# The scale of ScalarE's linear factor from a register in place of a pointer operand

## The chip, the cores and the metric

The kernel runs on one core of a Trainium2 chip. The time is that of the device in microseconds (us), from runs of the whole program; less is better. The engines are TensorE (PE; its weight loads are PEld), VectorE (DVE), ScalarE (ACT), GpSimd (POOL) and SyncE (SP). Each has its own queue of instructions and runs it in order; the engines wait for each other by semaphores.

## The reference

A polynomial attention is followed by a layer with a rational activation. Attention has 4 batches of 4 heads, 1088 tokens and a head width of 32, so the layer sees 4352 tokens of width 128 and has 2048 hidden columns.

```python
def phi(x):
    a = np.einsum('rd,bhsd->bhsr', S1, x)
    b = np.einsum('rd,bhsd->bhsr', S2, x)
    return np.einsum('bhsi,bhsj->bhsij', a, b).reshape(*x.shape[:-1], r * r)
q_p, k_p = (phi(q), phi(k))
kv = np.einsum('bhsf,bhsd->bhfd', k_p, v)
z = np.sum(k_p, axis=2)
num = np.einsum('bhsf,bhfd->bhsd', q_p, kv)
den = np.einsum('bhsf,bhf->bhs', q_p, z)[..., None] + 1e-06
...
h = x @ w_in
h2 = h * h
h3 = h2 * h
P = a[0] + a[1] * h + a[2] * h2 + a[3] * h3
Q = 1.0 + np.abs(b[0]) * np.abs(h) + np.abs(b[1]) * h2
g = P / (Q + 1e-06)
return (g @ w_out).astype(np.float32)
```

## The kernel before, in words

Nothing loops on the chip: the program is a straight list of instructions, written out by the string `ORDER`, one step per word (`name:index`), and each engine gets its part of the steps in that order. Two kinds of work are interleaved. The attention part makes, per batch, the summed key products (`kvz`) and then, per block of some 384 queries, the attention output, transposed into `xT`. The layer part takes 17 units, numbered 0 to 16, of 4096 columns (a unit is a stretch of tokens times a share of the 2048 hidden columns, laid side by side), most of them worked on in two halves of 2048 columns, the last in a half and two quarters of 1024.

The steps of a unit:

- `h` (L455, TensorE): the product of `w_in` and `xT` into the PSUM tile `h_ps` of 1024 columns, of which there are two; `e` (L461, ScalarE) copies it to `hh` in SBUF as bf16.
- `u`, `w`, `y` (L484, L490, L495, VectorE): |h| and then w = |h| (|b1| |h| + |b0|), so that the denominator is 1 + w.
- `ln` (L546) and `ex` (L550), both on ScalarE: r = exp(-ln(1 + 1e-6 + w)), the reciprocal of the denominator.
- `pa` (L541, ScalarE) or `pd` (L536, VectorE): the linear factor p = a3 h + a2. The table `P_ON_ACT` says for each half which engine makes it: ScalarE makes 23 of them, 21 of 2048 columns and 2 of 1024, VectorE 12.
- `s`, `m`, `v`, `x` (L554, L558, L564, L569, VectorE): s = h r and the terms with h s and p, in the tile `g`.
- `G` (L588, TensorE): r, s and g times three copies of `w_out` scaled by a0, a1 and 1 (made once, in the steps `wo`, L621 to L625), summed over the hidden columns in PSUM; `st` (L597, L605) transposes the sum and stores it.

The four values of a lie in `a_sb`, a tile of 128 partitions by 4 in which every partition holds the same four numbers (it is fetched by a DMA that reads the four numbers 128 times); the two of b lie in `b_sb`, fetched next on the same queue. `a1`, `a2` and `a3` are columns of `a_sb`, one value per partition. In `a_p` ScalarE's instruction therefore reads two operands of one value per partition beside its data: the scale a3 and the bias a2. The activations of `ln` and `ex` have constants in their place.

The step `ba` stands once in `ORDER`, between `kp0` and `kp1` of the first batch; there ScalarE takes the absolute values of b (L682). The next ScalarE step behind it is `kk`, the copies of the key products into `kvz` (L312).

Of the kernel before, what the change touches and what calls it, by code (L numbers as in the profile page):

```python
# [15 lines left out]
ACT = mybir.ActivationFunctionType  # L16
# [53 lines left out]
def kernel(  # L70
# [13 lines left out]
    nc = tc.nc  # L84
# [54 lines left out]
    for i, s_in in enumerate((S1, S2)):  # L139
# [5 lines left out]
                      in_=bass.AP(tensor=k.tensor, offset=k.offset, ap=[[S * D // 32, 128], [W, NM], [1, 4 * D]]))  # L145
    nc.sync.dma_start(out=k0[:, 0:km].rearrange("p (m x) -> p m x", m=NM - 1)[:, :, 4 * D:],
                        in_=k0_src[:, 0:km].rearrange("p (m x) -> p m x", m=NM - 1)[:, :, 4 * D:])
# [4 lines left out]
    a_sb = consts.tile([128, 4], FP, name="a_sb")  # L152
# [14 lines left out]
    def turn(i, cols=512):  # L167
        idle_ps = bank()
        for _ in range(TURNS[i]):
            nc.tensor.matmul(idle_ps[:, :cols], lhsT=idle[:, 0:128], rhs=idle[:, :cols], start=True, stop=True)  # L170
# [45 lines left out]
    b_abs = consts.tile([128, 2], FP, name="b_abs")  # L216
    ab0, ab1 = b_abs[:, 0:1], b_abs[:, 1:2]
    a1, a2, a3 = a_sb[:, 1:2], a_sb[:, 2:3], a_sb[:, 3:4]
    w_sb = [big.tile([128, nf, d_model], BF, name=f"w_out_{i}") for i in range(3)]
    XR = 2048  # L220
    xT = big.tile([d_model, XR], FP, name="xT")
# [277 lines left out]
    def part_of(i, key, h):  # L499
        n = 2 if key == "p" else 4  # L500
        t = rings[key].rearrange("p n x -> p (n x)")
        if h == "both":
            return t[:, 2 * i % n * HW:2 * i % n * HW + UW]
        z = (2 * i + (h > 0)) % n * HW
        return t[:, z + (h - 2) * PW:z + (h - 1) * PW] if h > 1 else t[:, z:z + HW]
# [9 lines left out]
    def on_act(i, h):  # L515
        return P_ON_ACT[2 * i + (h > 0)]

    def skip(wide=(), same=None):
        def wrap(f):
            def step(i, h):  # L520
                if i in wide and i not in QUARTER and (same is None or same(i, 0) == same(i, 1)):
                    if h != 1:
                        return
                    h = "both"
                if h in (0, "both") or (h > 1) == (i in QUARTER):
                    f(i, h, live[i]["hh"][:, span(h)])
            return step
        return wrap

    def first(h):  # L530
        return 0 if h == "both" else h
# [6 lines left out]
    @skip(WIDE_P, on_act)  # L538
    def a_p(i, h, hh):
        if on_act(i, first(h)):  # L540
            nc.scalar.activation(out=part_of(i, "p", h), in_=hh, func=ACT.Identity, scale=a3, bias=a2)  # L541

    @skip()
    def a_ln(i, h, hh):
# [47 lines left out]
    def store(i):  # L592
        t0, tl, f0, per = units[i]
        if f0 + per < nf:
            return
        o = mid.tile([128, TC], FP, name="out_sb")
        nc.vector.transpose(out=o[:, :tl], in_=outs[t0][:, :tl])  # L597
        c = t0
        while c < t0 + tl:
            b = c // S  # L600
            ce = min(t0 + tl, (b + 1) * S)
            o_b = out[b * S:(b + 1) * S, :].rearrange("(g j) d -> g j d", g=32)
            j0, j1 = (c - b * S) // 32, (ce - b * S) // 32
            for e in range(d_model // 32):
                (nc.scalar if t0 + tl == n_tok and e % 2 else nc.sync).dma_start(  # L605
                    out=o_b[:, j0:j1, e * 32:(e + 1) * 32],
                    in_=o[e * 32:(e + 1) * 32, c - t0:ce - t0].rearrange("p (j d) -> p j d", d=32))
            c = ce
# [8 lines left out]
    def w_part(x):  # L617
        y, f = x // 2, x % 2 * (nf // 2)
        o, t = w_sb[y][:, f:f + nf // 2], w_out_sb_f[:, f:f + nf // 2]
        if y == 2:  # L620
            (nc.scalar.copy if W_ENG[x] else nc.vector.tensor_copy)(out=o, in_=t)  # L621
        elif W_ENG[x]:
            nc.scalar.activation(out=o, in_=t, func=ACT.Copy, scale=a_sb[:, y:y + 1])
        else:
            nc.vector.tensor_scalar(out=o, in0=t, scalar1=a_sb[:, y:y + 1], scalar2=None, op0=AX.mult)  # L625
# [26 lines left out]
    def fetch_x(x):  # L652
# [5 lines left out]
    blocks = [lambda: QA, lambda: QB, lambda: QC, once(lambda: Spread(0, q0, cuts[3], cuts[4]))]  # L658
    blocks += [once(lambda b=b, c0=c0, c1=c1: Spread(b, fetched["lq", b], c0, c1)) for b in range(1, B) for c0, c1 in spans]
    does = {"e": evac, "h": hidden, "u": d_abs, "w": d_w, "y": d_y, "ln": a_ln, "ex": a_exp, "pa": a_p, "pd": d_p,  # L660
            "s": d_s, "m": d_hs, "v": d_v, "x": d_g, "G": gather}
    q_does = {"qt": "transposes", "qs": "sketches", "qc": "copies", "qf": "features", "qp": "products", "qd": "plus",
# [5 lines left out]
    for step in ORDER:  # L668
        name, i = step.split(":")
        i = int(i)  # L670
        if name in q_does:
            getattr(blocks[i](), q_does[name])()
        elif name in k_does:
            getattr(keys[i](), k_does[name][0])(*k_does[name][1:])
        elif name == "wo":
            w_part(i)
        elif name in loads:
            fetched[name, i] = loads[name](i)
        elif name == "tn":
            turn(i)  # L680
        elif name == "ba":
            nc.scalar.activation(out=b_abs, in_=b_sb, func=ACT.Abs)  # L682
        elif name == "st":
            store(i)
        else:
            does[name[:-1]](i, int(name[-1]))
# [31 lines left out]
```

## Time and profile before

| | us |
|---|---|
| median of 3 runs | 272.32 |
| runs from, to | 272.06, 272.9 |
| span of the profiled execution, from its first instruction to its last | 270.8 |
| busy TensorE, VectorE, ScalarE in that span | 257.7, 256.7, 248.8 |
| the 23 instructions of L541 together | 46.7 |

The profile is that of one execution; no other time of that execution is given than its span, and the span is 1.5 us below the median of the runs. Its lines name the source line (L541), the engine, the operation and out<-in by the program's names, with partitions x elements and types. In a group, "x21" is the number of instructions, then come the busy time in us and the mean duration of one in ns, then the idle time of the engine just before them and what ended it. In a timeline a line starts with the start and the duration in us. A recorded duration reaches past the start of the next instruction on the same engine by up to about 0.1 us, so the distance between starts is the better measure of what an instruction costs its engine.

### The profile page before, as it was taken

Reading aid. Unit: us, or ns where it says so; the run is one execution under the profiler, and the core shown is the slowest. Engines: PE = TensorE matmul, PEld = TensorE weight load, DVE = VectorE, ACT = ScalarE, POOL = GpSimd, SP = SyncE. Lnnn points to the kernel's source line nnn. Section 1 sums busy time; section 2 is a strip of 40 time slices with the busy share of each in tenths; the row PEclk is TensorE's granted clock in tenths of the full one; section 3 lists DMA queues with packets and bytes.
Section 4 is the critical chain, followed back from the end, with each engine's and each line's share of the span. In section 5 each row is a group of like instructions: output and inputs, shape, how many; then the busy total and the mean of one; then the engine's idle time right before and its main releaser. Section 6 shows DMA issues by size and latency. Waiting matters only on the chain.

```text
span 270.8 us, 3732 instructions
## 1 busy us (share of the span) xinstructions
PE 257.7 (95%) x1382; PEld 147.5 (54%) x1397; DVE 256.7 (95%) x278; ACT 248.8 (92%) x224; POOL 2.9 (1%) x24
## 2 busy tenths in 40 slices
PE   8999999999999899999999999999999999999683
PEld 3787556864645344635464554444545356675372
DVE  3777999999999999999999999999999999999994
ACT  1268999998999999999999999999999999999991
POOL 4000000000000000000000000000000000000000
PEclk9999999999999999999999999999999999999889
DMA  6995614333230044231304000400034200020005
GB/s 167 265 323 151 156 38 136 117 90 96 76 106 34 12 118 100 77 75 33 97 6 123 7 0 3 119 11 0 15 97 73 43 0 0 2 39 1 0 2 79
DMA packets 30530, 19.55 MB, mean 72 GB/s; under 512 B 20400, under 2 KB 26672, under 8 KB 30512
## 3 DMA queue, kind: packets, MB, share of 16 engines
q1 hardware_dynamic: 28864, 18.92, 26.9%
q10 hardware_dynamic: 1648, 0.40, 0.8%
q8 instruction: 11, 0.18, 0.3%
q14 instruction: 7, 0.06, 0.1%
HBM read 16.16 MB, written 3.15 MB: 71 GB/s over the span
## 4 chain that ended last, share of the span: by engine, by line
ACT 47%; PE 34%; issue 8%; DVE 5%; DMA 4%; SPq 0%; ACTq 0%; DVEq 0%
PE h_ps L455 16%; ACT ln L546 13%; ACT r L550 12%; ACT hh L461 12%; PE att_ps L588 10%; ACT p L541 7%; PE att_ps L365 3%; DMA v_sb<-in_v_dram 2%; PE att_ps L302 2%; DMA k_sb<-in_k_dram 2%; DVE g L558 2%; DVE s L554 1%; ACT xT L398 1%; PE att_ps L391 1%; PE att_ps L409 1%
## 5 line engine op out<-in xcount | busy, mean ns | idle before, releaser
L455 PE MATMUL h_ps<-xT,w_in_sb 128*128 128x512 f32 (+1 forms) x320 | 125.8, 537 | 2.8 <-ACT hh L461 1.9
L455 PEld LDWEIGHTS h_ps<-xT,w_in_sb 128*128 128x128 f32 x320 | 58.3, 190 | 55.2 <-issue 37.3
L461 ACT CAST hh<-h_ps 128x1024 bf16<-128x1024 f32 x68 | 67.5, 1027 | 3.5 <-PE h_ps L455 3.1
L588 PEld LDWEIGHTS <-w_out 128*128 128x128 bf16 x460 | 45.5, 100 | 45.9 <-issue 14.3
L546 ACT ACTIVATE ln<-w 128x2048 f32<-128x2048 bf16 (+1 forms) x35 | 66.0, 1887 | 0.7 <-DVE w L495 0.6
L550 ACT ACTIVATE r<-ln 128x2048 bf16<-128x2048 f32 (+1 forms) x35 | 65.8, 1880 | 0.6 <-PE att_ps L588 0.2
L541 ACT ACTIVATE p<-hh,a_sb 128x2048 bf16<-128x2048 bf16 (+1 forms) x23 | 46.7, 2035 | 0.1
L554 DVE TENSOR_TENSOR s<-hh,r 128x2048 bf16<-128x2048 bf16 (+2 forms) x33 | 41.0, 1246 | 0.2 <-ACT r L550 0.2
L495 DVE TENSOR_TENSOR w<-w,u 128x4096 bf16<-128x4096 bf16 (+2 forms) x22 | 39.4, 1798 | 0.1
L588 PE MATMUL att_ps<-g,w_out 128*128 128x512 bf16 (+1 forms) x154 | 34.8, 350 | 4.3 <-DVE g L569 3.9
L558 DVE TENSOR_TENSOR g<-hh,s 128x2048 bf16<-128x2048 bf16 (+1 forms) x30 | 35.2, 1175 | 0.0
L569 DVE TENSOR_TENSOR g<-g,p 128x2048 bf16<-128x2048 bf16 (+1 forms) x30 | 35.1, 1178 | 0.1
L588 PE MATMUL att_ps<-r,w_out 128*128 128x512 bf16 (+1 forms) x154 | 34.8, 353 | 0.3
L588 PE MATMUL att_ps<-s,w_out 128*128 128x512 bf16 (+1 forms) x137 | 29.3, 342 | 0.2
L490 DVE TENSOR_SCALAR w<-u,b_abs 128x4096 bf16<-128x4096 bf16 (+2 forms) x22 | 23.8, 1090 | 0.0
L484 DVE TENSOR_SCALAR u<-hh 128x4096 uint16<-128x4096 uint16 (+2 forms) x22 | 21.4, 976 | 1.6 <-ACT hh L461 1.5
L365 PEld LDWEIGHTS att_ps<-kvz,q_pT 128*128 128x128 f32 x144 | 17.7, 191 | 4.6 <-issue 2.0
L365 PE MATMUL att_ps<-kvz,q_pT 128*128 128x66 f32 x144 | 17.9, 273 | 0.1
L302 PEld LDWEIGHTS att_ps<-v_sb,k_p 128*64 128x64 f32 (+1 forms) x288 | 8.8, 138 | 1.9 <-DVE qT L325 0.8
L536 DVE TENSOR_SCALAR p<-hh,a_sb 128x2048 bf16<-128x2048 bf16 x12 | 9.7, 808 | 0.0
L302 PE MATMUL att_ps<-v_sb,k_p 128*64 128x64 f32 (+1 forms) x288 | 9.2, 223 | 0.5 <-DMA v_sb<-in_v_dram 0.5
L273 DVE TENSOR_TENSOR k_p<-att_ps,b_sk 128x1024 f32<-128x1024 f32 (+2 forms) x8 | 9.3, 1178 | 0.1
(60 smaller groups left out, 134.3 us busy)
## 6 DMA issues: line engine op xcount, KB each, us to landing
a_all<-sk_d SPq DMA_DIRECT2D x6, 384.0 KB
b_all<-sk_d SPq DMA_DIRECT2D x12, 192.0 KB
v_sb<-in_v_dram SPq DMA_DIRECT2D x12, 144.0 KB
k_sb<-in_k_dram SPq DMA_DIRECT2D x3, 544.0 KB
q_sb<-in_q_dram SPq DMA_DIRECT2D x3, 544.0 KB
a_all<-sk_d SPq DMA_DIRECT2D x4, 320.0 KB
b_all<-sk_d SPq DMA_DIRECT2D x8, 160.0 KB
w_out_sb_f<-in_moe_w_out_dram SPq DMA_DIRECT2D x2, 512.0 KB
```

The costliest lines, as they stand in the source:

```text
L365: nc.tensor.matmul(self.nd[:, o:o + 2 * KW], lhsT=self.q_p[:, c, x:x + 128], rhs=kvz[self.b % 2][:, c, :], start=True, stop=True)
L455: nc.tensor.matmul(t[:, x * tl:(x + 1) * tl], lhsT=w_in_sb[:, f * 128:(f + 1) * 128], rhs=xT[:, x_at(t0):x_at(t0) + tl], start=True, stop= ...
L461: nc.scalar.copy(out=live[i]["hh"][:, part * PW:(part + 1) * PW], in_=live[i]["h", part])
L490: nc.vector.tensor_scalar(out=t[:, c], in0=live[i]["u"][:, c], scalar1=ab1, scalar2=ab0, op0=AX.mult, op1=AX.add)
L495: nc.vector.tensor_mul(out=t[:, c], in0=t[:, c], in1=live[i]["u"][:, c])
L541: nc.scalar.activation(out=part_of(i, "p", h), in_=hh, func=ACT.Identity, scale=a3, bias=a2)
L546: nc.scalar.activation(out=t, in_=live[i]["w"][:, span(h)], func=ACT.Ln, bias=1.0 + 1e-6)
L550: nc.scalar.activation(out=part_of(i, "r", h), in_=live[i]["ln"], func=ACT.Exp, scale=-1.0)
L554: nc.vector.tensor_mul(out=part_of(i, "s", h), in0=hh, in1=part_of(i, "r", h))
L558: nc.vector.tensor_mul(out=part_of(i, "g", h), in0=hh, in1=part_of(i, "p" if horner(i, first(h)) else "s", h))
L569: nc.vector.tensor_mul(out=g, in0=g, in1=part_of(i, "s" if horner(i, first(h)) else "p", h))
L588: nc.tensor.matmul(outs[t0][:, :tl], lhsT=w_sb[y][:, f0 + x, :], rhs=part_of(i, key, h)[:, c:c + tl], start=done[0] == 0, stop=done[0] == ...
```

## The change

One register of ScalarE is allocated. In the step `ba`, behind the absolute values of b, it is loaded with the 32 bits of a3 from the first partition of `a_sb`. The activation in `a_p` takes its scale from that register; its bias a2 stays an operand of one value per partition. VectorE's form of the same factor (`d_p`), the order of the steps and all DMAs stay.

```diff
@@ -216,6 +216,7 @@
     b_abs = consts.tile([128, 2], FP, name="b_abs")
     ab0, ab1 = b_abs[:, 0:1], b_abs[:, 1:2]
     a1, a2, a3 = a_sb[:, 1:2], a_sb[:, 2:3], a_sb[:, 3:4]
+    a3_reg = nc.scalar.alloc_register("a3_reg")
     w_sb = [big.tile([128, nf, d_model], BF, name=f"w_out_{i}") for i in range(3)]
     XR = 2048
     xT = big.tile([d_model, XR], FP, name="xT")
@@ -538,7 +539,7 @@
     @skip(WIDE_P, on_act)
     def a_p(i, h, hh):
         if on_act(i, first(h)):
-            nc.scalar.activation(out=part_of(i, "p", h), in_=hh, func=ACT.Identity, scale=a3, bias=a2)
+            nc.scalar.activation(out=part_of(i, "p", h), in_=hh, func=ACT.Identity, scale=a3_reg, bias=a2)
 
     @skip()
     def a_ln(i, h, hh):
@@ -680,6 +681,7 @@
             turn(i)
         elif name == "ba":
             nc.scalar.activation(out=b_abs, in_=b_sb, func=ACT.Abs)
+            nc.scalar.reg_load(a3_reg, a_sb[0:1, 3:4].bitcast(mybir.dt.int32))
         elif name == "st":
             store(i)
         else:
```

## The prediction

> **What bounds the kernel now.** I read first the page's busy times, then busy time by stretch of the span, then the chain of waits, then who waits for whom, and last the timelines of ScalarE and VectorE. The first fence has the page's busy line, the two stretches 20 to 248 us and 248 to 271 us (busy us of each engine, in brackets its instructions), and the chain by engine and by line.
>
> ```profile
> span 270.8 us, 3732 instructions
> PE 257.7 (95%) x1382; PEld 147.5 (54%) x1397; DVE 256.7 (95%) x278; ACT 248.8 (92%) x224; POOL 2.9 (1%) x24
> 20.00:248.00 228.00, 224.38 (x1121) 123.90 (x1135) 224.98 (x225) 225.52 (x196) 0.00 (x0) 1.00 0.24 61
> 248.00:271.00 23.00, 15.01 (x99) 10.16 (x98) 18.76 (x23) 16.03 (x12) 0.00 (x0) 0.93 0.16 24
> ACT 47%; PE 34%; issue 8%; DVE 5%; DMA 4%; SPq 0%; ACTq 0%; DVEq 0%
> by line: PE h_ps L455 16.2%; ACT ln L546 13.0%; ACT r L550 12.1%; ACT hh L461 12.1%; PE att_ps L588 10.2%; issue 8.1%; ACT p L541 7.4%; PE att_ps L365 3.1%; DMA v_sb<-in_v_dram 2.4%; PE att_ps L302 1.7%; DMA k_sb<-in_k_dram 1.6%; DVE g L558
> ```
>
> The page's 92% for ScalarE hides the point. Its idle time lies at the start and the end; in the 228 us between, ScalarE is idle for 228.00 - 225.52 = 2.5 us, VectorE for 3.0 and TensorE for 3.6. Three engines are full there. The chain of waits therefore crosses between them: 47% ScalarE, 34% TensorE. After 248 us VectorE has the most work (18.76 us, ScalarE 16.03).
>
> Next, who waits for whom from 20 to 250 us (total us, times, longest).
>
> ```profile
> PE h_ps L455 <- ACT hh L461: 1.9, 4, 0.8
> PE h_ps L455 <- ACT xT L398: 0.4, 1, 0.4
> DVE u L484 <- ACT hh L461: 1.5, 2, 0.9
> DVE rec L380 <- ACT den L376: 0.9, 2, 0.5
> DVE s L554 <- ACT r L550: 0.2, 1, 0.2
> ACT hh L461 <- PE h_ps L455: 3.1, 3, 1.7
> ACT r L550 <- PE att_ps L588: 0.2, 1, 0.2
> ```
>
> VectorE loses 1.5 + 0.9 + 0.2 = 2.6 us to ScalarE, TensorE 1.9 + 0.4 = 2.3 us, and ScalarE itself loses 3.3 us to TensorE. That is all that a faster ScalarE could take from the other two, and part of it lies where no earlier ScalarE instruction is touched.
>
> **The change part by part: the pointer removed.** Here are ScalarE's groups with shapes kept apart: busy us, mean ns of one, idle before.
>
> ```profile
> L541 ACT ACTIVATE p<-hh,a_sb 128x2048 bf16<-128x2048 bf16 x21 | 44.3, 2112 | 0.1
> L546 ACT ACTIVATE ln<-w 128x2048 f32<-128x2048 bf16 x33 | 63.9, 1937 | 0.6 <-DVE w L495 0.6
> L541 ACT ACTIVATE p<-hh,a_sb 128x1024 bf16<-128x1024 bf16 x2 | 2.4, 1226 | 0.0
> L550 ACT ACTIVATE r<-ln 128x1024 bf16<-128x1024 f32 x2 | 2.1, 1051 | 0.0
> L623 ACT ACTIVATE w_out<-w_out_sb_f,a_sb 128x1024 bf16<-128x1024 f32 x2 | 2.3, 1156 | 0.0
> L621 ACT CAST w_out<-w_out_sb_f 128x1024 bf16<-128x1024 f32 x1 | 1.1, 1070 | 0.0
> ```
>
> p (L541) reads two pointers, the scale a3 and the bias a2; ln and r have constants alone. The difference is 2112 - 1937 = 175 ns on 2048 columns and 1226 - 1051 = 175 ns on 1024: a fixed price of two pointers, whatever the width. One pointer alone shows in the w_out pair, which differ in a pointer scale on the same shape: 1156 - 1070 = 86 ns. So the price adds up pointer by pointer, and 175 / 2 = 88 ns is what one p should lose. There are 21 + 2 = 23 of them: 23 x 88 ns = 2.0 us of ScalarE's time. No row shows a scale from a register, so this value stands between two ends: the register is as cheap as a constant (-2.0 us in all) or handled as dearly as the pointer or more (0 and above, the third rival). I take the first, because the value is known to the engine's queue before the instruction starts and no SBUF read of 128 values is left.
>
> The saving must also be in the distance between starts and not only in the recorded length, since neighbours overlap:
>
> ```profile
> 246.02 2.10 ACT L541 ACTIVATE p<-hh,a_sb 128x2048 bf16<-128x2048 bf16 x1
> 248.02 1.91 ACT L546 ACTIVATE ln<-w 128x2048 f32<-128x2048 bf16 x1
> 207.49 1.93 ACT L546 ACTIVATE ln<-w 128x2048 f32<-128x2048 bf16 x1
> 209.30 1.01 ACT L461 CAST hh<-h_ps 128x1024 bf16<-128x1024 f32 x1
> 201.93 1.91 ACT L546 ACTIVATE ln<-w 128x2048 f32<-128x2048 bf16 x1
> 203.87 1.91 ACT L550 ACTIVATE r<-ln 128x2048 bf16<-128x2048 f32 x1
> ```
>
> From p to the next start 2.00 us pass, from an ln to an independent next start 1.81 us: 0.19 us for two pointers, so the whole price is in the pitch. The third pair (r needs ln) has 1.94 us: where the next instruction can't overlap, 0.13 us are lost.
>
> **How much of 2.0 us reaches the end.** The chain has 7.4% of 270.8 us on p, 20.0 us, or 10 instructions of 2.0 us. Were the chain to stay where it is, the end would move by 10 x 88 ns = 0.88 us; with the other engines full it switches sooner, so 0.88 us is the upper end of the likely case. The lower end is 0. Two places show both signs:
>
> ```profile
> 246.90 1.22 DVE L558 TENSOR_TENSOR g<-hh,s 128x2048 bf16<-128x2048 bf16 x1
> 248.16 1.23 DVE L558 TENSOR_TENSOR g<-hh,p 128x2048 bf16<-128x2048 bf16 x1
> 162.14 0.23 DVE L380 RECIPROCAL rec<-den 128x12 f32<-128x12 f32 x1 [0.38 <-ACT den L376]
> 158.27 1.98 PE L455 MATMUL h_ps<-xT,w_in_sb 128*128 128x512 f32 x4 [0.44 <-ACT hh L461]
> 91.95 5.80 PE L455 MATMUL h_ps<-xT,w_in_sb 128*128 128x512 f32 x12 [0.85 <-ACT hh L461]
> ```
>
> At 248.16 VectorE starts the product with p as p ends (246.02 + 2.10 = 248.12), 0.04 us after its own work at 246.90 + 1.22 = 248.12, where neighbours normally overlap by 0.08: at most 0.12 us is to be had there. At 162.14 (0.38 us idle, 0.46 with the overlap) and 158.27 (0.44 us) VectorE and TensorE do wait for ScalarE, so what ScalarE has gained by then passes on. But VectorE's idle time there and what lies behind it leave little: 0.46 + 0.12 is what I find from 158 us on, and of the earlier waits (91.95 among them) I count some 0.2 us, since hh is late from TensorE, too (3.1 us of waits), and each such place takes ScalarE's lead away again. Sum as an upper figure: 0.2 + 0.46 + 0.12 = 0.78 us; as each wait gives only what ScalarE leads by then, I take two thirds: 0.5 us. That is 270.8 - 0.5 = 270.3 us of span. The profiled span is 1.5 us below the median of the runs, 272.32 us; with the same 1.5 us around it the forecast is 271.8 us.
>
> **The register load added.** It is one instruction on ScalarE's queue, behind b_abs (L682). No row shows such a load. Nearest rows: a sequencer-only semaphore event (51 ns), and ScalarE's only other load of its own state, the table load (1283 ns). What stands behind it on the queue is the copy into kvz:
>
> ```profile
> 10.12 0.21 ACT L682 ACTIVATE b_abs<-b_sb 128x2 f32<-128x2 f32 x1
> 12.34 0.54 ACT L312 COPY kvz<-att_ps 64x33 f32<-64x33 f32 x4 [2.02 <-PE att_ps L302]
> L455 PEldq EVENT_SEMAPHORE  x5: 51/51/51, 16.8 to 218.5; - x5
> L158 ACT ACT_TABLE_LOAD x1 | 1.3, 1283 | 3.6 <-DMA s_raw<-in_S_dram 3.6
> ```
>
> kvz waits 2.02 us for TensorE's products, so both ends, 0.05 and 1.28 us, are hidden: 0. Without that cover the load's own length would go on ScalarE's path, up to 1.28 us, and the copy to kvz, then TensorE's first query products, would be late. a_sb was fetched before b_sb on the same queue, so no new DMA wait arises. The Trainium skill, Runtime: NRT & Kernel Launch, section Instruction fetch mechanics, gives some 200 ns for one register loaded from HBM; by that figure the load is hidden as well, and no run here shows it.
>
> No wait is added to any p: the register is written once, on the engine that reads it. The DMAs, the order and the other queues stay as they are.
>
> **The rivals.**
>
> 1. *More comes through* (faster). ScalarE leads for longer than I give it: the waits of 2.6 and 2.3 us on ScalarE are large enough to take all of 2.0 us, and 47% of the chain is on ScalarE. Against it: the chain has only 10 of 23 p's, and VectorE's 18.76 us after 248 us don't hang on ScalarE. It gives 0.9 to 2.0 us, say 1.2: 271.1 us.
>
> 2. *The register costs what the pointer cost* (no change). The edit then does not do what it is said to, as ScalarE handles both forms alike: 272.3 us. If the bits were read as an integer, the time would be the forecast's and the output wrong.
>
> 3. *The register form cannot be prepared behind its predecessor* (slower). Fetching the register's value then falls between two activations, at each of the 23 p's on a full engine. The price: the overlap lost, 0.13 us, and one sequencer step, 0.05 us, against 0.088 us saved: +0.09 us each, 23 x 0.09 = 2.1 us. It decides from 0.088 us per p. As ScalarE has 2.5 us idle in 228, nearly all of it would be on the path, say 1.7 us: 274.0 us. A far end is a DMA issue on ScalarE's queue (two in 0.88 us, so 0.44 each): 23 x 0.35 = 8.1 us. For it: no row has this form. Against it: ScalarE starts tiny copies 0.06 us after the one before, so its queue is filled ahead.
>
> ```profile
> 42.22 0.19 ACT L376 ACTIVATE den<-att_ps 128x12 f32<-128x12 f32 x1
> 42.28 1.07 ACT L621 CAST w_out<-w_out_sb_f 128x1024 bf16<-128x1024 f32 x1
> 267.62 0.88 ACTq L605 DMA_DIRECT2D out_dram<-out_sb  x2
> ```
>
> The Trainium skill's Perfetto Trace Analysis, section Sequencer Loop, says that an engine instruction is pushed into a queue and only rarely gets special work in the sequencer's own code. A register operand may be such a rare case: with it the sum would be that of this rival, and without it that of the forecast. The 0.06 us between starts above bear out the queue, and no row of before bears out the special work.
>
> 4. *The load isn't hidden*: it takes longer than 2.02 us or holds up the start in another way, about 1.3 us: 273.6 us.
>
> **How the numbers follow.** Forecast (0.5 us less) 0.45; more comes through 0.25; register as dear as the pointer 0.12; slower by lost overlap 0.15; load in the way 0.03. The time is the forecast's, 271.8 us; its own range is 271.1 to 272.5. The range that holds 8 in 10 takes in most of the first rival (to 1.6 us less: 270.7) and the nearer half of the third (to 1.5 us more: 273.8). About 0.3%, 0.8 us, is what a measurement of this kernel tells from no change: three runs of before spread over 0.84 us. Faster by more than that: 0.23 of the first rival, 0.05 of the forecast's upper end and 0.02 by scatter, 0.30. Slower: 0.14 + 0.03 and 0.03 by scatter, 0.20. Within: 0.50.
>
> **What would show it right or wrong.** In the changed profile the 21 wide p's should have a mean near 2024 ns and the two narrow ones near 1138; a start-to-start distance of 1.91 us after p. If p stays at 2112 ns, rival 2 holds; if the mean falls but the gap before p grows, or its idle before rises from 0.1 us to over 1 us, rival 3. ScalarE's busy time should fall by 2.0 us to 246.8, and its idle from 20 to 248 us rise by about 1.5 us, put down to TensorE or VectorE: that is the part absorbed. kvz should still start at 12.3 us, waiting for TensorE; a start past 13 us is rival 4. A span below 269.9 us, or VectorE's waits on ScalarE falling by over 1 us, would mean that I underrated what passes on.

## The result and the profile after

| | before | after |
|---|---|---|
| median, us | 272.34 (8 runs, 272.06 to 272.9) | 271.81 (8 runs, 271.45 to 272.05) |
| ratio, 95% interval | | 0.9972 [0.9961, 0.9982] |
| profiled execution: its time, its span, us | not given, 270.8 | 272.05, 270.3 |
| L541 (after: L542), 23 instructions together, us | 46.7 | 44.5 |

The medians differ by 0.53 us. The ratio of the runs says 0.28%, which is 0.76 us, with 0.49 to 1.06 us as its interval; where comparisons are set beside each other below, it is by the ratio. The source lines behind the first edit are one higher than before, those behind the register load two.

First the page of the changed kernel and its two stretches 20 to 248 us and 248 to 271 us (busy us of each engine, in brackets its instructions; then the clock, the DMA share and GB/s).

```profile
span 270.3 us, 3749 instructions
PE 257.8 (95%) x1397; PEld 147.5 (55%) x1397; DVE 256.2 (95%) x278; ACT 247.2 (91%) x224; POOL 2.9 (1%) x24
20.00:248.00 228.00, 224.98 (x1139) 124.22 (x1138) 225.08 (x226) 224.91 (x197) 0.00 (x0) 1.00 0.24 61
248.00:271.00 23.00, 14.78 (x98) 9.98 (x96) 18.17 (x22) 15.07 (x11) 0.00 (x0) 0.87 0.16 24
PE 44%; ACT 25%; DVE 15%; issue 7%; DMA 6%; SPq 1%; DVEq 0%; ACTq 0%
PE h_ps L456 21%; PE att_ps L589 17%; ACT hh L462 8%; ACT ln L547 8%; ACT r L551 6%; DVE s L555 3%; DMA w_in_sb<-in_moe_w_in_dram 3%; DVE w L496 3%; ACT p L542 3%; PE att_ps L366 2%; DVE g L559 2%; DMA q_sb<-in_q_dram 2%; DVE g L570 1%; DVE w L491 1%; DVE k_p L274 1%
```

The chain has moved: ScalarE's share falls from 47% to 25%, TensorE's rises from 34% to 44%, VectorE's from 5% to 15%. ScalarE's busy time falls by 1.6 us; in it, records that overlap count once. Next ScalarE's groups (busy us, mean ns of one, idle before).

```profile
L547 ACT ACTIVATE ln<-w 128x2048 f32<-128x2048 bf16 x33 | 63.9, 1937 | 0.8 <-DVE w L496 0.7
L542 ACT ACTIVATE p<-hh,a_sb 128x2048 bf16<-128x2048 bf16 x21 | 42.4, 2017 | 0.2 <-DVE g L570 0.2
L542 ACT ACTIVATE p<-hh,a_sb 128x1024 bf16<-128x1024 bf16 x2 | 2.2, 1132 | 0.0
```

p loses 2112 - 2017 = 95 ns and 1226 - 1132 = 94 ns; ln stays. 23 x 95 ns = 2.2 us of ScalarE's time, of which 0.53 us show in the median and 0.76 us in the ratio. The waits from 20 to 250 us (total us, times, longest) say where some of the rest went.

```profile
PE h_ps L456 <- ACT hh L462: 1.9, 4, 0.7
PE h_ps L456 <- ACT xT L399: 0.4, 1, 0.4
DVE rec L381 <- ACT den L377: 0.6, 2, 0.4
ACT hh L462 <- PE h_ps L456: 4.2, 5, 2.3
ACT p L542 <- DVE g L570: 0.2, 1, 0.2
```

VectorE's waits on ScalarE are down from 2.6 to 0.6 us; ScalarE's own waits on TensorE are up from 3.3 to 4.2 us, and a wait of p on VectorE is new. Much of both belongs to the start, where the DMAs land differently in each execution: from 30 us on, VectorE's waits on ScalarE go from 1.1 to 0.6 us, and ScalarE's on TensorE from 0.9 to 1.2. So I compared the two timelines instruction by instruction. The two fences show the places that matter, ScalarE's and VectorE's timelines (start us, duration us, ..., idle before).

```profile
35.86 1.01 ACT L462 CAST hh<-h_ps 128x1024 bf16<-128x1024 f32 x1 [0.30 <-PE h_ps L456]
72.19 2.00 ACT L542 ACTIVATE p<-hh,a_sb 128x2048 bf16<-128x2048 bf16 x1 [0.18 <-DVE g L570]
200.33 1.01 ACT L462 CAST hh<-h_ps 128x1024 bf16<-128x1024 f32 x1 [0.17 <-PE h_ps L456]
245.44 2.01 ACT L542 ACTIVATE p<-hh,a_sb 128x2048 bf16<-128x2048 bf16 x1
```

```profile
161.72 0.23 DVE L381 RECIPROCAL rec<-den 128x12 f32<-128x12 f32 x1 [0.18 <-ACT den L377]
246.40 1.22 DVE L559 TENSOR_TENSOR g<-hh,s 128x2048 bf16<-128x2048 bf16 x1
247.54 1.22 DVE L559 TENSOR_TENSOR g<-hh,p 128x2048 bf16<-128x2048 bf16 x1
```

The reciprocal that stood at 162.14 us with 0.38 us idle before it stands at 161.72 with 0.18: VectorE has taken over 0.2 us of lead there. The product with p that began 1.26 us after its predecessor (246.90, 248.16) now begins 1.14 us after it (246.40, 247.54): the 0.12 us that the prediction found there are had in full. On the other side ScalarE loses 0.33 us at 35.86 and hands back about 0.09 us at 72 us and at some later places, 0.19 us around 201 us. From the first p (22.37 and 22.50 us) to the start of the last (263.56 and 262.75, worked out from the starts) ScalarE gains 0.93 us of its 2.1, and the end of the span, which VectorE and TensorE make, gains less: 0.13 us were behind at the first p, and ScalarE's lead in the last microseconds serves nobody.

The 0.33 us at 35.86 us are not a lead handed back: the load-alone run below, whose p are as long as before, has the same loss (0.41 us idle at 35.43 us). It comes from the start of the execution, here in the profile of the changed kernel:

```profile
21.95 1.37 DVE L255 STREAM_TRANSPOSE kT<-k_sb 128x224 f32<-128x224 f32 x2 [2.48 <-DMA k_sb<-in_k_dram]
25.92 1.03 DVE L326 STREAM_TRANSPOSE qT<-q_sb 128x384 f32<-128x384 f32 x2
27.10 0.55 PE L410 MATMUL att_ps<-qT,S 128*64 128x192 f32 x4 [0.38 <-ACT xT L399]
```

VectorE waits 2.48 us for the DMA of k (0.22 us at this step in the profile of before), its transposes of q end at 26.95 us, and TensorE's products with them start 0.15 us later, after 0.38 us of idle time. In the load-alone run that idle time is 0.56 us, again 0.15 us behind the end of the transposes; in the profile of before there is none. The profile puts the wait down to the copy of xT, but before, the same products start at 26.52 us, ahead of that copy at 26.62.

Last the load (first row: duration min/median/max, then first and last start) and its neighbours in ScalarE's timeline.

```profile
L684 ACTq TENSOR_LOAD <-a_sb x1: 481/481/481, 9.4 to 9.4; - x1
```

```profile
9.41 0.59 ACT L346 COPY a_all<-h_ps 128x512 f32<-128x512 f32 x1 [0.78 <-PE h_ps L339]
9.90 0.21 ACT L683 ACTIVATE b_abs<-b_sb 128x2 f32<-128x2 f32 x1
11.91 0.55 ACT L313 COPY kvz<-att_ps 64x33 f32<-64x33 f32 x4 [1.81 <-PE att_ps L303]
```

The load takes 0.48 us and starts at 9.4 us, while the copy to a_all is at work and ahead of b_abs, which stands before it on the queue: the queue is worked off ahead of the engine. It ends as b_abs starts. b_abs starts 0.49 us behind the copy, as in the profile of before (9.63 and 10.12 us), and kvz still waits 1.81 us for TensorE, so the load delays nothing here.

### The profile page after: what moved, and what is told of

Read it like the earlier page. It is cut to its first block, busy times and chain, and to the rows that moved or that the text cites. A ratio compares the mean times of both kernels' runs of the same rounds, so it can differ in the third digit from the quotient of the medians.

```text
span 270.3 us, 3749 instructions
## 1 busy us (share of the span) xinstructions
PE 257.8 (95%) x1397; PEld 147.5 (55%) x1397; DVE 256.2 (95%) x278; ACT 247.2 (91%) x224; POOL 2.9 (1%) x24
## 4 chain that ended last, share of the span: by engine, by line
PE 44%; ACT 25%; DVE 15%; issue 7%; DMA 6%; SPq 1%; DVEq 0%; ACTq 0%
PE h_ps L456 21%; PE att_ps L589 17%; ACT hh L462 8%; ACT ln L547 8%; ACT r L551 6%; DVE s L555 3%; DMA w_in_sb<-in_moe_w_in_dram 3%; DVE w L496 3%; ACT p L542 3%; PE att_ps L366 2%; DVE g L559 2%; DMA q_sb<-in_q_dram 2%; DVE g L570 1%; DVE w L491 1%; DVE k_p L274 1%
## 5 line engine op out<-in xcount | busy, mean ns | idle before, releaser
L542 ACT ACTIVATE p<-hh,a_sb 128x2048 bf16<-128x2048 bf16 (+1 forms) x23 | 44.5, 1940 | 0.2 <-DVE g L570 0.2
L589 PE MATMUL att_ps<-g,w_out 128*128 128x512 bf16 (+1 forms) x160 | 35.9, 353 | 3.7 <-DVE g L570 3.7
L589 PE MATMUL att_ps<-r,w_out 128*128 128x512 bf16 (+1 forms) x160 | 36.0, 355 | 0.0
L589 PE MATMUL att_ps<-s,w_out 128*128 128x512 bf16 (+1 forms) x140 | 29.9, 343 | 0.0
L255 DVE STREAM_TRANSPOSE kT<-k_sb 128x224 f32<-128x224 f32 (+4 forms) x10 | 5.9, 617 | 3.7 <-DMA k_sb<-in_k_dram 3.7
```

What stands on the lines that cost most here:

```text
L589: nc.tensor.matmul(outs[t0][:, :tl], lhsT=w_sb[y][:, f0 + x, :], rhs=part_of(i, key, h)[:, c:c + tl], start=done[0] == 0, stop=done[0] == ...
```

## The experiments

They ran in three sets; each set has its own runs of the kernel before, whose medians were 272.69, 272.71 and 272.85 us, so ratios and not times are compared between sets. A "lead" is worked out from starts of the same instruction in two timelines.

**Is the load free?** The scale goes back to the pointer and the line of the load stays.

```diff
-            nc.scalar.activation(out=part_of(i, "p", h), in_=hh, func=ACT.Identity, scale=a3_reg, bias=a2)
+            nc.scalar.activation(out=part_of(i, "p", h), in_=hh, func=ACT.Identity, scale=a3, bias=a2)
```

> The register is loaded and nothing reads it; the scale is the pointer again. Theory (the load is hidden and the whole gain comes from the shorter p): p at 2112 ns as before, the load at some 0.48 us, kvz still waits for TensorE, time 272.3 us, ratio within 0.1% of 1. Rival (the load or the one instruction more moves the start, for good or ill): p at 2112 ns and a time more than 0.3 us away from 272.3 us.

272.79 us, ratio 1.0008 [0.9999, 1.0016]; ScalarE's group of p, what the trace has at the line of the load (duration min/median/max in ns, then first and last start), and a place in ScalarE's timeline:

```profile
L542 ACT ACTIVATE p<-hh,a_sb 128x2048 bf16<-128x2048 bf16 x21 | 44.3, 2111 | 0.1
```

```profile
L684 ACTq EVENT_SEMAPHORE  x1: 17/17/17, 9.1 to 9.1; - x1
```

```profile
35.43 1.01 ACT L462 CAST hh<-h_ps 128x1024 bf16<-128x1024 f32 x1 [0.41 <-PE h_ps L456]
```

The experiment did not do what it was meant to. Nothing reads the register, and the trace has no load: at its line stands a semaphore event of 17 ns, where every trace of a kernel that reads the register has the load. So the run is a repetition of the kernel before, and says nothing of the load. It is of use as that: the median is 0.1 us off, but from the first p to the last it takes 241.55 us in the profile, where before takes 241.19. Two profiles of the same work differ by 0.36 us, and the loss at 35.43 us accounts for that. That the load costs nothing rests on the trace of the changed kernel above and on the next experiment, in which the kernel with the load is no slower than the one without.

**Is a register as cheap as a constant?** Twice: in the first set the constant alone, in the third the constant beside the changed kernel itself.

```diff
-            nc.scalar.activation(out=part_of(i, "p", h), in_=hh, func=ACT.Identity, scale=a3, bias=a2)
+            nc.scalar.activation(out=part_of(i, "p", h), in_=hh, func=ACT.Identity, scale=0.25, bias=a2)
```

> The scale of ScalarE's linear factor is the constant 0.25, no register, no load; the factor is computed with 0.25 in place of a3. Theory (a register is as cheap as a constant): p at 2017 ns on 2048 columns and 1132 on 1024, time 271.8 us, as with the register. Rival (the register form has a price of its own beside the recorded length, which eats part of the gain): p at 2017 ns or less and a time of 271.3 us or below.

> The changed kernel itself, beside a run with the constant scale on the same chip and with the same runs of the kernel before. Theory (the register costs what a constant costs): its ratio to the kernel before and that of the next run agree within 0.1%. Rival (the register form has a price that p's length doesn't show): 0.3% or more slower than the next run.

> The scale is the constant 0.25 in place of a3, no register and no load: the partner of the run before. Theory: 0.997 of the kernel before, within 0.1% of the run before. Rival: 0.994 or less.

The constant: 271.5 us, 0.9961 [0.9948, 0.9974], and again 271.72 us, 0.996 [0.9947, 0.9974]. The register beside it: 271.57 us, 0.9953 [0.994, 0.9967]. Here the register's group of p and, in the second fence, the constant's of the same set:

```profile
L542 ACT ACTIVATE p<-hh,a_sb 128x2048 bf16<-128x2048 bf16 x21 | 42.3, 2015 | 0.2 <-DVE g L570 0.2
L542 ACT ACTIVATE p<-hh,a_sb 128x1024 bf16<-128x1024 bf16 x2 | 2.2, 1132 | 0.0
```

```profile
L541 ACT ACTIVATE p<-hh,a_sb 128x2048 bf16<-128x2048 bf16 x21 | 42.3, 2015 | 0.2 <-DVE g L569 0.2
L541 ACT ACTIVATE p<-hh,a_sb 128x1024 bf16<-128x1024 bf16 x2 | 2.2, 1132 | 0.0
```

The two forms are the same to the nanosecond, and from the start of the first p to the end of the last activation both kernels take 241.05 us, to within 0.01 us (before: 242.42). A register costs what a constant costs, and the gain is that of the shorter p. The first run of the constant had missed its expected 271.8 us in the direction of the rival; in one set, register and constant differ by 0.15 us, the register being the faster, so the form has no hidden price.

The repetition shows more. The register gains 1.28 us in this set, the constant 1.06 and 1.09 us, all by the ratio; the first comparison gave 0.76. A gain of 0.9 to 1.06 us lies in all four intervals. In the profile of the repetition the 0.33 us at 35.86 us aren't lost (first p to last activation: 241.05 us, against 241.39 in the first profile). Set beside a profile of the pointer with the same start, the two profiles of the register agree: from the first p to the last, the first takes 1.29 us less than the load-alone run (241.55 and 240.26 us), which has the loss at 35 us as well, and the repetition 1.27 us less than before (241.19 and 239.92), and neither of these two has it. To the end of the span it is 1.1 and 1.0 us from the first p. The other places are the same in both: 72, 106, 118, 201 and 217 us.

**Does a second saving bring as much?** The bias becomes a constant, too.

```diff
-            nc.scalar.activation(out=part_of(i, "p", h), in_=hh, func=ACT.Identity, scale=a3, bias=a2)
+            nc.scalar.activation(out=part_of(i, "p", h), in_=hh, func=ACT.Identity, scale=0.25, bias=0.0)
```

> Scale and bias of the factor are constants (0.25 and 0), so the factor is 0.25 h. Theory (ScalarE's time is handed back where TensorE or VectorE is last): p near 1937 ns if the second pointer goes as well, 23 x 80 ns = 1.8 us less of ScalarE's time than with the register, of which 0.1 to 0.4 us reach the end: 271.4 to 271.7 us. Rival (all of ScalarE's savings beyond the first pass on, since ScalarE is what the others wait for): 270.0 us. If a bias of 0 is read through a pointer as well, p stays at 2017 ns and the time at 271.8 us.

271.77 us, 0.9971 [0.9958, 0.9983], with a wide scatter (270.89 to 272.74). ScalarE's group, and rows of the timeline:

```profile
L541 ACT ACTIVATE p<-hh 128x2048 bf16<-128x2048 bf16 x21 | 40.4, 1922 | 0.3 <-DVE g L569 0.3
L541 ACT ACTIVATE p<-hh 128x1024 bf16<-128x1024 bf16 x2 | 2.0, 1041 | 0.0
```

```profile
112.54 0.55 PE L391 MATMUL att_ps<-ident,x_tok 128*128 128x128 f32 x3 [0.51 <-ACT xT L398]
113.13 0.43 ACT L398 COPY xT<-att_ps 128x320 f32<-128x320 f32 x1 [0.64 <-PE att_ps L391]
```

The second pointer costs as much as the first, 2015 - 1922 = 93 ns, and ScalarE has another 2.1 us less to do; of these nothing shows in the median. In the profile the lead over the register's run of the third set is 0.46 us at 112 us, in spite of a loss at 35 us like the one above, and is lost at one stroke, where TensorE's transposes (L391) and ScalarE's copies of them to xT wait for each other. Why they do so here and not in the register's run, where the transposes start before the copies, is open.

**The other direction.** The kernel before, with 35 more pointer reads.

```diff
+    ones = consts.tile([128, 1], FP, name="ones")
+    nc.gpsimd.memset(ones, 1.0)
...
-        nc.scalar.activation(out=t, in_=live[i]["w"][:, span(h)], func=ACT.Ln, bias=1.0 + 1e-6)
+        nc.scalar.activation(out=t, in_=live[i]["w"][:, span(h)], func=ACT.Ln, scale=ones, bias=1.0 + 1e-6)
```

> The other direction: the kernel before, in which the 35 logarithms take a scale of 1 through a pointer to a tile of ones, so ScalarE has 35 x 95 ns = 3.3 us more. Theory (three engines are full, and ScalarE has 2.5 us idle in the middle): a loss costs more per us than a gain brings; ln at 2032 ns, 1.6 to 3.0 us of the 3.3 reach the end, 273.9 to 275.3 us. Rival (a fixed share of 0.53 / 2.18 = 24% of ScalarE's time shows at the end, in both directions): 273.1 us.

274.95 us, 1.0085 [1.0073, 1.0097], so 2.3 us slower. ScalarE's groups:

```profile
L548 ACT ACTIVATE ln<-w,ones 128x2048 f32<-128x2048 bf16 x33 | 66.8, 2025 | 0.5 <-DVE w L497 0.5
L548 ACT ACTIVATE ln<-w,ones 128x1024 f32<-128x1024 bf16 x2 | 2.3, 1150 | 0.1
```

A pointer costs 2025 - 1937 = 88 ns here, 33 x 88 + 2 x 93 ns = 3.1 us in all; 74% of it reach the end (64 to 85% by the interval), where of the 2.2 us saved some 40 to 50% do (0.9 to 1.06 us). So a microsecond more on ScalarE cost more here than a microsecond less brought. That the direction makes the difference is argued and not shown: the pointer was added to ln and taken from p, and r waits for each ln.

**Who takes the lead back?** Two pairs in which other engines have less to do, each with the pointer and with the register. In the first, the sum over the hidden columns leaves out its middle term (TensorE less); in the second VectorE's product w times |h| is left out as well.

```diff
-        return [[(x, y, key) for x in range(*c)] if y != 1 or not horner(i, n) else []
+        return [[(x, y, key) for x in range(*c)] if y != 1 else []
...
-        t = live[i]["w"]
-        nc.vector.tensor_mul(out=t[:, c], in0=t[:, c], in1=live[i]["u"][:, c])
+        return
```

> Pointer scale, and the sum over the hidden columns leaves out its middle term: TensorE has 137 of its matmuls less (29.3 us busy by the group s of L588), ScalarE and VectorE as before. It is the base for the next run. Theory (three engines are full): 0.5 to 2.5 us faster than the kernel before, 270.2 to 272.2 us, because VectorE and ScalarE stay full; TensorE no longer makes hh wait in the middle. Rival (TensorE sets the end, as it has the largest part of the chain after the change): 5 us faster or more.

> The same without the middle term, with the register scale. Theory A (TensorE is the one that takes back ScalarE's lead): against the run with the pointer scale 1.0 to 1.8 us are gained in place of 0.5. Theory B (VectorE, full by itself, takes it back): 0.3 to 0.8 us, as with the whole sum.

> Pointer scale; the middle term of the sum is left out and so is VectorE's product w times |h| (L495, 39.4 us of VectorE), so that the denominator lacks its square. ScalarE alone has a full queue. Base for the next run; theory: ScalarE's 248.8 us of busy time and the start and the end bound it: 258 to 268 us.

> The same two parts left out, with the register scale. Theory (what ScalarE saves is whole, 23 x 95 ns = 2.2 us, and is lost only to the other full engines): against the pointer scale 1.7 to 2.2 us are gained. Rival (the register form costs ScalarE something that its recorded length doesn't show): 1.2 us or less, although ScalarE alone is full.

| | ratio to the kernel before | median, us | all runs, us |
|---|---|---|---|
| less TensorE, pointer | 1.0097 [1.0064, 1.013] | 275.77 | 273.61 to 278.31 |
| less TensorE, register | 1.0051 [1.0025, 1.0076] | 273.80 | 272.34 to 276.15 |
| less of both, pointer | 1.0141 [1.0106, 1.0176] | 277.11 | 272.9 to 277.18 |
| less of both, register | 1.0097 [1.0061, 1.0133] | 274.58 | 271.33 to 276.86 |

Both bases missed: with less to do, the kernel is slower, and each of the four scatters over 4 to 6 us. What differs is the granted clock of TensorE (span and mean clock), here of the first base, and of the changed kernel in the second fence:

```profile
core 0: 273.6 us, clock 0.969
```

```profile
core 0: 270.3 us, clock 0.990
```

Within the first base the time goes with it: 273.61 us at 0.980, 275.35 at 0.969, 276.43 at 0.962, 278.31 at 0.957. In these traces the clock is either full or half, and the first base has stretches of half clock of some 3.4 us in the middle, where the changed kernel has none from 20 to 254 us. Here is one (busy us of TensorE, its weight loads, VectorE, ScalarE and GpSimd, then the clock), and what follows in ScalarE's timeline; in the register's run of the pair the same stretch has the clock 1.00.

```profile
55.20:58.60 3.40, 3.40 (x15) 2.38 (x14) 3.05 (x5) 2.31 (x4) 0.00 (x0) 0.50 0.11 29
```

```profile
58.98 0.48 ACT L398 COPY xT<-att_ps 128x384 f32<-128x384 f32 x1 [1.45 <-PE att_ps L391]
```

ScalarE loses 1.56 us to the register's run at this place, more than the whole gain of the change. All twelve runs with the register and less TensorE have 0.956 to 0.975, so the medians and the ratios compare clocks and say little of the register. Of the first pair, runs of the same clock (0.968 and 0.969) take 275.12, 275.35 and 276.19 us with the pointer, 274.06, 274.36, 274.49 and 274.88 with the register: means 275.55 and 274.45, 1.1 us apart, from few runs that scatter by as much. In the second pair the runs don't go by the clock alone: at 0.981 the pointer takes 272.90 us, but the register takes 271.33 us at 0.978 and 275.13 at 0.980, so by the clock it is 1.6 us faster or 2.2 us slower. What is left for this pair are its profiles: from the first p to the last ScalarE takes 1.54 us less with the register. Theories A and B stay undecided, and that the gain grows with less on the other engines is not shown: about 1 us is what the whole kernel gains, too, and 1.54 us stands against 1.27 with the whole kernel, mostly because nothing is lost at 201 us. 2.2 us are not reached in that profile, though the stretch 20 to 248 us of the last kernel leaves VectorE 37 us idle and TensorE 18:

```profile
20.00:248.00 228.00, 210.38 (x1035) 114.16 (x1034) 191.16 (x205) 224.76 (x197) 0.00 (x0) 0.99 0.24 62
```

The small losses at 72, 106, 118 and 217 us are there as before, 0.09 to 0.10 us each. They don't come from full engines, then, but from the order of the work. At 72 us p waits for VectorE's product. At 217 us (the same kernel's timeline):

```profile
212.65 3.70 PE L456 MATMUL h_ps<-xT,w_in_sb 128*128 128x512 f32 x8 [0.44 <-ACT hh L462]
213.37 2.04 ACT L541 ACTIVATE p<-hh,a_sb 128x2048 bf16<-128x2048 bf16 x1
215.33 2.06 ACT L462 CAST hh<-h_ps 128x1024 bf16<-128x1024 f32 x2
```

TensorE waits 0.44 us for a hh to free a tile and then needs 3.70 us for eight products; the second of the two hh behind p waits for the last of them. That round, from hh over TensorE to hh, runs past p, and a shorter p only makes hh wait longer at its end. At 106 and 118 us hh likewise waits at the end of a run of TensorE without a gap. The loss at 201 us is not in this pair, in which TensorE and VectorE have time to spare, nor is the one at 35.86.

**Where along the program?**

```diff
-            nc.scalar.activation(out=part_of(i, "p", h), in_=hh, func=ACT.Identity, scale=a3_reg, bias=a2)
+            nc.scalar.activation(out=part_of(i, "p", h), in_=hh, func=ACT.Identity, scale=a3_reg if i > 8 else a3, bias=a2)
```

> The register scale is used in the units 9 to 16 alone, the pointer in 0 to 8. Theory (the lead builds up along the whole program, and each place hands back its own part): p at 2112 ns early and 2017 late, no lead before 140 us, then the lead of the full change from there on, 0.4 to 0.5 us at the last p; 0.2 to 0.5 us in the median. Rival (the gain hangs on the last place alone, where VectorE waits for p at 248 us): 0.1 us.

272.39 us, 0.9988 [0.9979, 0.9997], 0.33 us by the ratio. By ScalarE's starts there is no lead up to 151 us and 0.50 us at the last p; the full change has in the same set 1.27. The 11 late p's bring some 0.05 us each in lead, the 12 early ones 0.06.

**What does a load cost that isn't covered?** The load is repeated in front of every p.

```diff
+            nc.scalar.reg_load(a3_reg, a_sb[0:1, 3:4].bitcast(mybir.dt.int32))
             nc.scalar.activation(out=part_of(i, "p", h), in_=hh, func=ACT.Identity, scale=a3_reg, bias=a2)
```

> The register is loaded anew in front of each of the 23 linear factors, 23 x 0.48 us = 11 us of loads on ScalarE's queue. Theory (ScalarE's queue is filled ahead, and a load in it runs while the activations before it are still at work): nearly all hidden, 271.8 to 273.5 us, p at 2017 ns. Rival (a load lies between two activations, as a step that the queue must finish first): 4 us or more above the kernel before, 276 to 284 us.

272.71 us, 0.9994 [0.9985, 1.0003]: 1.14 us above the register loaded once, in the same set. The loads (duration min/median/max in ns), and a place in ScalarE's timeline:

```profile
L542 ACTq TENSOR_LOAD <-a_sb x23: 273/276/482, 21.3 to 262.1; - x23
```

```profile
111.60 0.19 ACT L377 ACTIVATE den<-att_ps 128x12 f32<-128x12 f32 x1
111.92 2.00 ACT L543 ACTIVATE p<-hh,a_sb 128x2048 bf16<-128x2048 bf16 x1
```

24 loads are written, the one in `ba` and 23 more; the first is overwritten before it is read, and the trace has 23, with a semaphore event of 17 ns at the line of the one in `ba`. They take 6.7 us, and about a sixth of it shows. Behind the short den p starts 0.32 us after den, in the register's run 0.06 us (110.43 and 110.49): the load of 0.28 us ends at 111.83, so it is not covered there. Of the 23 it is the only one that keeps p waiting; in front of the others the distance from the instruction before to p is that of the register's run to 0.01 us. Where the rest of 1.14 us comes from is open. The profiled execution, of 273.98 us the slowest of the twelve, doesn't say: of the 1.4 us that ScalarE is behind the register's run in it, 1.2 arise before 37 us, where TensorE waits 1.28 us for VectorE's transposes of q, as in the start described above. Mostly the queue is filled ahead by more than a load takes.

## Why the prediction was right

- *The price of a pointer.* 88 ns were read off the pairs of groups; 95 were measured by removing one, 93 by removing the second. The sum of ScalarE's savings was 2.0 us, and is 2.2.
- *The register as cheap as a constant.* Taken between two ends; the constant beside the register shows it. Rivals 2 and 3 fall: p is 95 ns shorter, and nothing is added in front of it.
- *The load hidden.* Bounds 0.05 and 1.28 us, measured 0.48, and b_abs and kvz start in the trace as without it. Rival 4 falls. The figure in the Trainium skill, Runtime: NRT & Kernel Launch, section Instruction fetch mechanics, some 200 ns a register from HBM, is of the order of the 276 ns that a repeated load from SBUF took here.
- *How much reaches the end.* 0.5 us was the forecast, and 0.53 the difference of the medians. That close a hit is in part luck. The ratio of the same runs says 0.76 us, and the four comparisons in which p loses one pointer agree on 0.9 to 1.06 us, about twice the forecast: above the 0.88 us that the prediction called the upper end of the likely case, and at the lower end of its first rival (0.9 to 2.0). At 162 and 248 us the steps were right in kind (0.2 us of the 0.46 and all of the 0.12 us pass to VectorE at these places). But "some 0.2 us" for the waits before 158 us was too small: in the third set ScalarE leads by 0.74 us at 151 us. The step said that each place where TensorE is last "takes ScalarE's lead away again"; the timelines show that such a place takes 0.09 us or so of it, about one p's saving, and leaves the rest, since TensorE itself had moved up at the places where it waits for hh.
- *The signs.* Two of those that the prediction named for having underrated this term came, if narrowly: VectorE's waits on ScalarE fell by 2.0 us, 0.5 of it after 30 us, and the span of the third set's profile is 269.88 us, below 269.9.
- *The idle that should appear on ScalarE.* About 1.5 us were to be handed back from 20 to 248 us. ScalarE's idle time there rises from 2.5 to 3.1 us in the first profile and to 2.8 in the third set's. Counted place by place 0.9 us are lost in the first profile (0.33 of it by the start) and 0.6 in the third set's, and from ScalarE's last activation to the end of the span 6.03 us have become 6.38 and 6.44, so that another 0.4 us at most are lost behind it.

## What to carry to other kernels

A scale that all partitions share can be given to ScalarE from a register, which costs what a constant does; it saved some 95 ns at each instruction here, at 1024 columns as at 2048. The load is best put once, where the engine waits anyway. Where several engines are full, expect a part of such a saving at the end, here not quite half, and find it by going through the places at which another engine waits for this one and those at which this one waits: a lead is not cancelled by a wait, it is shortened by what the other engine has not gained. Before an effect of half a per cent is put down to the edit, repeat both kernels in another set of runs, and compare profiles whose starts are alike. Before a run is said to test an instruction, find that instruction in its trace.

## What the runs showed of the hardware that was not expected

Taking 140 matmuls from TensorE (the trace of before, which misses some, has 137 of them) made the kernel slower by 0.97%: the granted clock fell from 0.99 to between 0.957 and 0.980, in the trace by stretches of half clock, two of them of some 3.4 us in the middle of the program, and single executions spread over 4 us. A ScalarE register load from SBUF took 276 ns when repeated and 481 ns the first time. A load whose register nothing reads is not in the trace at all.
